# A hand-ordered attention and SwiGLU kernel: its first quarter in another order, its last two project units woven

## The chip, the cores and the metric

One core of one Trainium2 chip. The time is device microseconds of one execution of the program; three executions of the kernel before give the median. TensorE multiplies into PSUM, ScalarE (ACT) and VectorE (DVE) read PSUM and compute element by element, GpSimd (POOL) and SyncE (SP) issue DMAs. In the profile PE is TensorE's matmuls and PEld its weight loads.

## What is computed

Eight batches of attention with eight heads of 576 queries and 64 elements, 16 beacon keys ahead of the 576 causal ones, then a SwiGLU layer on the 4608 tokens of 512 elements:

```python
k_all = np.concatenate([beacon_k, k], axis=2)
v_all = np.concatenate([beacon_v, v], axis=2)
scores = scale * np.matmul(q, k_all.transpose(0, 1, 3, 2))
causal[:, Nb:] = np.triu(np.ones((S, S), dtype=bool), k=1)
scores = np.where(causal, -1000000000.0, scores)
a = np.exp(scores - scores.max(-1, keepdims=True)); a /= a.sum(-1, keepdims=True) + 1e-09
x = np.matmul(a, v_all)            # heads side by side: 4608 x 512
g = x @ w_gate                     # 512 x 1536
out = (g * (1.0 / (1.0 + np.exp(-g))) * (x @ w_val)) @ w_out
```

## The kernel before, in words

Everything is in bf16 with fp32 sums. Matmuls that contract 128 elements are cut into two row halves of 64 partitions, which TensorE takes side by side; `halves` issues them. PSUM is four slots of two banks each. `take` hands the slot that has been free longest to whoever asks next, `give` returns one, so a piece may wait for the piece that had its slot before. Where a bank changes from one row half to the other, `halves` puts a wait for the last matmul of that slot ahead ("one bank, two row halves").

The order of all work is written out by hand, as a string of letters, `plan` (L806). The loop at its end takes a letter after the other and calls `piece`, which issues the next instance of that kind of work; each engine then runs its own instructions in that order. The letters that matter here:

- `l`, a load from the list `order_of_loads`, issued by POOL. The first 24 are free; each later one stands behind a wait for the TensorE work of two pieces before (`passed[-2]`, L739). `K0.4` is batch 0's keys of heads 4 to 7, `K1` all of batch 1's, `Q` the queries, `v1.3` a part of batch 1's values, `g2` and `u2` parts of the gate and value weights (wg, wv), `o0` of w_out, `b1` beacons.
- `f`, `g`: pair_up, a copy of loaded keys and queries into the order that a turn needs, on POOL or on DVE. `T`: a turn, transposes of queries and keys on TensorE. Turns 0 to 4 are of batch 0, 5 to 8 of batch 1, 9 to 12 of batch 2. `K k Q q`: copies of a turn out of PSUM, capitals on DVE, small letters on ACT.
- `S`, `s`: scores of a unit (A to D of a head pair) with, for `s`, the causal mask added on TensorE. `E`: their exponential on ACT, which frees the slot. `D`, `M`: causal masks on DVE or POOL.
- `P`, `p`: product with the values; in batches 0 to 3 with all 128 rows at once. `R`: its normalization on DVE. `X y`: turn and copy of x; `V`: the same by DMA on SP.
- `G`, `H`: the halves of a gate-and-value unit; then tanh on ACT (`a`) and two products on DVE (`1`, `2`). Units 0 to 5 take batch 0's first 240 tokens, 6 to 11 the next 272, later ones 512.
- `F`: a step of the projection with w_out, 24 steps for 256 tokens; `O`, `o`: its copy out of PSUM on DVE or ACT, with the store.
- `h`: a filler. The next scores or product that takes a slot first waits for it, and then issues a pair of matmuls of 128 columns into it for each `h` (`keep_warm`, L176), whose results are overwritten.

The last projection (of the last 256 tokens) is computed in two parts by columns, 0 to 383 and 384 to 511 (`CUT`), each part in slots of its own, one for each bank.

Of the kernel before, what the change touches and what calls it, by code (L numbers as in the profile page):

```python
# [868 lines left out]
```

## Time and profile before

| | us |
|---|---|
| three timed executions | 365.43, 365.43, 364.56 |
| median | 365.43 |
| span of the profiled execution | 362.0 |
| the profiled execution's own time | not listed |
| TensorE busy, matmuls | 352.9 (97%) |
| DVE, ACT, POOL busy | 225.4, 187.6, 124.6 |

The span is the time from the first to the last instruction of one profiled execution. Engines work side by side, so the shares don't add up. Matmuls overlap: a matmul of 512 columns is listed with 0.376 us, and a pair of them starts every 0.216 us, so a busy TensorE is not one at its peak. An idle time in a row stands behind the instruction in brackets, with what ended it.

### The profile page before, as it was taken

What the parts mean: (1) busy time and instruction counts of PE and PEld (TensorE: products, weight loads), DVE (VectorE), ACT (ScalarE), POOL (GpSimd) and SP (SyncE); (2) the same over time, 40 slices, a digit from 0 to 9 for tenths busy, and PEclk for the clock granted to TensorE, in tenths of its full rate; (3) what the DMA queues carried; (4) which work ended last, traced back from release to release, by engine and by line L of the source; (5) the groups of instructions that cost most, each with busy time, mean ns of one, the idle gap of its engine ahead of it and who ended that gap; (6) DMA issues with size and microseconds to landing.
All of it is one profiled execution on the core that took longest, in us unless ns stands there. A gap on an engine that the chain in (4) does not pass through costs nothing.

```text
span 362.0 us, 11888 instructions
## 1 busy us (share of the span) xinstructions
PE 352.9 (97%) x5160; PEld 198.6 (55%) x5160; DVE 225.4 (62%) x439; ACT 187.6 (52%) x284; POOL 124.6 (34%) x188
## 2 busy tenths in 40 slices
PE   7799999999999999999999999999999999999996
PEld 3587565654444566554565566546655554455544
DVE  5577997566766654487528754776467764464342
ACT  4966999723434777544863576447633232221310
POOL 8945499926247545374423013111000000000000
PEclk9999999999999999999999999999999999999999
DMA  8999999999999999999979829502413000110113
GB/s 121 156 197 204 191 191 158 174 175 147 149 147 121 134 136 129 153 174 135 122 132 147 109 37 154 67 6 26 113 62 65 2 2 0 61 60 1 61 60 116
DMA packets 146132, 39.74 MB, mean 110 GB/s; under 512 B 131488, under 2 KB 141728, under 8 KB 146080
## 3 DMA queue, kind: packets, MB, share of 16 engines
q0 software_dynamic: 97424, 19.00, 72.1%
q1 hardware_dynamic: 48368, 19.79, 27.9%
q8 instruction: 40, 0.66, 0.8%
q10 hardware_dynamic: 288, 0.20, 0.2%
q14 instruction: 12, 0.10, 0.1%
...
## 4 chain that ended last, share of the span: by engine, by line
PE 85%; DMA 5%; POOL 5%; DVE 2%; ACT 1%; issue 1%; POOLq 0%
PE gv_ps L168 49%; PE o_ps L168 25%; DMA qk<-in_q_dram 5%; PE s_ps L168 5%; PE pv_ps L168 4%; PE pv_ps L493 2%; POOL qk L209 2%; POOL vb L219 1%; DVE x L522 1%; POOL wg L248 1%; POOL wv L248 1%; DVE p L414 1%; PE t_ps L166 0%; ACT p L405 0%; ACT th L579 0%
## 5 line engine op out<-in xcount | busy, mean ns | idle before, releaser
L168 PE MATMUL gv_ps<-xT,wv 64*128 64x512 bf16 (+2 forms) x912 | 203.2, 365 | 0.0
L168 PE MATMUL gv_ps<-xT,wg 64*128 64x512 bf16 (+2 forms) x912 | 202.8, 365 | 0.1
L579 ACT ACTIVATE th<-gv_ps 128x512 f32<-128x512 f32 (+2 forms) x114 | 65.4, 575 | 116.5 <-PE gv_ps L168 116.1
L405 ACT ACTIVATE p<-s_ps 128x832 bf16<-128x832 f32 (+2 forms) x127 | 104.3, 868 | 32.4 <-PE s_ps L168 28.7
L168 PE MATMUL o_ps<-wo,hT 64*128 64x512 bf16 (+2 forms) x912 | 116.5, 365 | 0.2
L584 DVE SCALAR_TENSOR_TENSOR u<-th,gv_ps 128x512 f32<-128x512 f32 (+2 forms) x114 | 74.7, 656 | 65.9 <-ACT th L579 65.1
L168 PEld LDWEIGHTS <-wg 64*128 64x128 bf16 x912 | 82.5, 94 | 45.9 <-PE gv_ps L168 2.4
L168 PEld LDWEIGHTS <-wv 64*128 64x128 bf16 x912 | 81.8, 94 | 40.1 <-issue 0.7
L591 DVE SCALAR_TENSOR_TENSOR hT<-gv_ps,u 128x512 bf16<-128x512 f32 (+2 forms) x114 | 74.7, 661 | 3.0
L168 PEld LDWEIGHTS <-hT 64*128 64x128 bf16 x912 | 42.3, 94 | 34.1 <-PE o_ps L168 1.2
L219 POOL DMA_DIRECT2D vb<-in_v_dram x40 | 33.9, 853 | 64.1 <-PE s_ps L168 25.7
L168 PE MATMUL s_ps<-qT,kT 64*128 64x336 bf16 (+3 forms) x512 | 43.0, 250 | 1.9 <-ACT kT L256 1.0
L168 PEld LDWEIGHTS <-kT 64*128 64x128 bf16 x512 | 23.8, 94 | 22.9 <-ACT kT L256 1.8
L219 POOL DMA_DIRECT2D qk<-in_q_dram x25 | 21.2, 851 | 25.7 <-PE gv_ps L168 7.1
L414 DVE TENSOR_TENSOR p<-p,upper 128x256 bf16<-128x256 bf16 (+2 forms) x84 | 24.0, 317 | 9.8 <-ACT p L405 8.1
L522 DVE TENSOR_TENSOR x<-pv_ps,rec 128x640 bf16<-128x640 f32 (+1 forms) x32 | 25.3, 791 | 1.2
L521 DVE RECIPROCAL rec<-pv_ps 128x10 f32<-128x10 f32 (+1 forms) x32 | 6.8, 213 | 28.1 <-PE pv_ps L168 22.7
L258 DVE COPY o_sb<-o_ps 128x512 f32<-128x512 f32 (+2 forms) x20 | 12.7, 654 | 17.0 <-PE o_ps L168 13.9
L219 POOL DMA_DIRECT2D qk<-in_k_dram x25 | 21.3, 856 | 5.4 <-PE gv_ps L168 4.3
L418 POOL TENSOR_SCALAR_AFFINE_SELECT p<-p 128x256 bf16<-128x256 bf16 (+2 forms) x46 | 17.4, 399 | 14.0 <-ACT p L405 13.8
L168 PEld LDWEIGHTS <-p 64*128 64x128 bf16 x960 | 18.8, 94 | 4.5 <-PE pv_ps L168 0.2
L168 PE MATMUL pv_ps<-vb,p 64*128 64x65 bf16 x960 | 19.9, 189 | 0.0
...
## 6 DMA issues: line engine op xcount, KB each, us to landing
...
```

What stands on the lines that cost most here:

```text
L168: ins = nc.tensor.matmul(o, lhsT=l, rhs=r, start=start, stop=stop)
L209: return nc.gpsimd.dma_start(qk[b % 2][base : base + HALF, RUN * h0 : RUN * h1] .rearrange("p (h e) -> p h e", e=RUN)[:, :, D * i0 : D * i ...
L219: return nc.gpsimd.dma_start(dst[p0 : p0 + n, c, :, 0:D], src[b, :, r : r + n, :].rearrange("h j d -> j h d"))
L248: nc.gpsimd.dma_start(t[:, :, cols], src[:, cols].rearrange("(kk p) f -> p kk f", p=P))
L258: eng.tensor_copy(o, i)
L405: nc.scalar.activation(p_of(b, m, u == "A")[:, :, c0 : c0 + w], ps[:, :, 0:w], ACT.Exp, scale=0.125)
L414: nc.vector.tensor_tensor(out=ap, in0=ap, in1=upper[:, None, d : d + w].to_broadcast([P, 2, w]), op=ALU.mult)
L418: nc.gpsimd.affine_select(out=ap, in_=ap, compare_op=ALU.is_ge, fill=0.0, base=d, pattern=[[0, 2], [1, w]], channel_multiplier=-1,)
L522: nc.vector.tensor_tensor(out=xs[b][:, c0:NKT, P * m : P * m + P].rearrange("p c (h d) -> p h c d", d=D), in0=o[:, :, :, 0:D], in1=rec[:, ...
L579: nc.scalar.activation(th[:, 0:w], gvs[n][:, 0, 0:w], ACT.Tanh, scale=0.5)
L584: nc.vector.scalar_tensor_tensor(out=u[:, 0:w], in0=ths[n][:, 0:w], scalar=1.0, in1=gvs[n][:, 0, 0:w], op0=ALU.add, op1=ALU.mult)
L591: nc.vector.scalar_tensor_tensor(out=hTs[j][:, f, c0:c1], in0=gvs.pop(n)[:, 1, 0 : c1 - c0], scalar=0.5, in1=ths.pop(n)[:, 0 : c1 - c0], o ...
```

## The change

The fixed number of free loads goes; a new letter `L` is a free load, `l` always a paced one. The list of loads is reordered up to about its fiftieth entry. The plan is another one up to gate-and-value unit 23 (0-based), with the same pieces but 38 fillers in place of 10, and with some copies, masks and pair_ups on another engine (`A` and `Y` are beacon and x copies on DVE). After that the letters are the same up to the copies behind the last two project units, numbers 16 and 17, each of 24 steps. These two are woven: first half of 16, first half of 17's part 0, second half of 16, first half of 17's part 1, second half of part 0, second half of part 1. Part 0 now has 320 columns, and the two parts of 17 share a slot, one in each bank; for unit 17 the wait of `halves` looks at the bank alone and not at the slot.

```diff
@@ -50,7 +50,6 @@
 W_PARTS = [(0, 1), (1, 3), (3, 6), (6, 9), (9, 12)]
 
 
-FREE_LOADS = 24
 
 NHT = 2
 NPT = 3
@@ -151,16 +150,17 @@
     newest = [None]
     passed = []
 
-    def halves(key, bank, row, o, l, r, start, stop, turn=False):
+    def halves(key, bank, row, o, l, r, start, stop, turn=False, alone=False):
 
         at = (held[key], bank)
         was = writers.get(at)
         if was is not None and was[0] != row:
-            last = max((w for (i, _), w in writers.items() if i == at[0]), key=lambda w: w[2])
+            near = [w for w in writers if (w == at if alone else w[0] == at[0])]
+            last = max((writers[w] for w in near), key=lambda w: w[2])
             if was[3]:
                 after(nc.tensor.nop(), last[1], "one bank, two row halves")
             for other, w in writers.items():
-                if other[0] == at[0]:
+                if other in near:
                     writers[other] = (w[0], w[1], w[2], False)
         if turn:
             ins = nc.tensor.transpose(o, l, r)
@@ -595,33 +595,39 @@
         give(("g", n))
 
     projected = {}
-    CUT = 384
+    CUT = 320
+    LAST = NCH * 2 - 1
+    PARTS = (slice(0, CUT), slice(CUT, DM))
+
+    steps = [(pr, 0, f) for pr in range(LAST - 1) for f in range(2 * NF)]
+    for pr, part, half in (
+        (LAST - 1, 0, 0), (LAST, 0, 0), (LAST - 1, 0, 1), (LAST, 1, 0), (LAST, 0, 1), (LAST, 1, 1)
+    ):
+        each = 2 if pr == LAST else 1
+        steps += [(pr, part, f) for f in range(NF * half, NF * half + NF, each)]
 
     def project(n):
-        pr, s = divmod(n, 2 * NF)
+        pr, part, s = steps[n]
         j, i = divmod(2 * pr, TOK // P)
-        last = pr == NCH * 2 - 1
-        parts = [(0, slice(0, DM), s)]
-        if last:
-
-            parts = [(0, slice(0, CUT), 2 * s), (0, slice(0, CUT), 2 * s + 1)] if s < NF else [
-                (1, slice(CUT, DM), 2 * (s - NF)), (1, slice(CUT, DM), 2 * (s - NF) + 1)]
-        for part, cols, st in parts:
-            if st == 0:
+        last = pr == LAST
+        cols = PARTS[part] if last else slice(0, DM)
+        for st in range(s, s + 1 + last):
+            if st == 0 and part == 0:
                 for bank in range(2):
-                    key = ("f", pr, part, bank * last)
+                    key = ("f", pr, bank * last)
                     if key not in held:
                         ps = take(key, [P, 2, DM], FP32, "o_ps")
-                    projected[pr, part, bank] = key, ps
+                    projected[pr, bank] = key, ps
             second, f = divmod(st, NF)
             for row in (1, 0) if second else (0, 1):
                 bank = row ^ second
-                key, ps = projected[pr, part, bank]
+                key, ps = projected[pr, bank]
                 k64 = slice(HALF * row, HALF * row + HALF)
+                at = part if last else bank
                 halves(
-                    key, bank, row, ps[:, bank, cols],
+                    key, at, row, ps[:, at, cols],
                     hTs[j][k64, f, P * (i + bank) : P * (i + bank) + P], wo[k64, f, cols],
-                    st == 0, st == 2 * NF - 1,
+                    st == 0, st == 2 * NF - 1, alone=last,
                 )
 
     stored = {}
@@ -629,17 +635,17 @@
     def evacuate(n, eng):
 
         pr, bank = divmod(n, 2)
-        part, cols = 0, slice(0, DM)
-        if pr >= NCH * 2 - 1:
-            part, cols = pr - (NCH * 2 - 1), (slice(0, CUT), slice(CUT, DM))[pr - (NCH * 2 - 1)]
-            pr = NCH * 2 - 1
+        part, cols, at = 0, slice(0, DM), bank
+        if pr >= LAST:
+            part = at = pr - LAST
+            pr, cols = LAST, PARTS[part]
         r = 2 * P * pr + P * bank
         if part == 0:
             stored[pr, bank] = o_pool.tile([P, DM], FP32, name="o_sb")
         o_sb = stored[pr, bank]
-        key, ps = projected[pr, part, bank]
-        copy(eng, o_sb[:, cols], ps[:, bank, cols])
-        if bank == 1 or key[-1] != projected[pr, part, 1][0][-1]:
+        key, ps = projected[pr, bank]
+        copy(eng, o_sb[:, cols], ps[:, at, cols])
+        if part if pr == LAST else bank:
             give(key)
         (nc.sync if part == 0 or bank == 0 else nc.scalar).dma_start(out[r : r + P, cols], o_sb[:, cols])
 
@@ -718,24 +724,23 @@
         named[f"K0.{h}"] = lambda h=h: runs(0, k, h, h + 4, FRONT, ROWS)
         named[f"Q0.{h}"] = lambda h=h: runs(0, q, h, h + 4, FRONT, ROWS)
     order_of_loads = """
...
     """
     loads = [named[name] for name in order_of_loads.split()]
     assert sorted(order_of_loads.split()) == sorted(named)
     turns = [load for b in range(NPE, B) for load in dma_transposes(b)]
 
     def piece(kind):
-        as_kind = {"s": "S", "M": "D", "k": "K", "q": "Q", "Y": "y", "o": "O", "i": "I", "A": "e", "f": "g"}.get(kind, kind)
+        as_kind = {"s": "S", "M": "D", "k": "K", "q": "Q", "Y": "y", "o": "O", "i": "I", "A": "e", "f": "g", "L": "l"}.get(kind, kind)
         n = done.get(as_kind, 0)
         done[as_kind] = n + 1
-        if kind == "l":
-            if n >= FREE_LOADS:
-
+        if kind in "lL":
+            if kind == "l":
                 after(nc.gpsimd.nop(), passed[-2], "paced load")
             loads[n]()
         elif kind == "b":
@@ -804,25 +809,25 @@
     skipped = [0]
 
     plan = """
-    0lhbTqllhhWKeBhTQslTlEKlsqlkElhhSlTQsKElKEslssUQEshsEhDElshEEEllhlTQZkNZsNSPpJEEIlsJPllERIpSXlDR
...
-    FFFOFFFFOFFFOFFFFOFFFFFFFFOo
+    bLWLB0TQLTkAhhsETqKsqKhhSEThhhsLEELQKkLhsEhsQELhhhsTLQsLELKLELhhsEhhhZhhsUDhZNLhshhhSELsLNJIEhhS
...
+    FFFF1FFFFF2oFFFFFFFFFFFFOFFFFFFFOFoFFFFFFFFFFFOoFFFFFFOo
     """
```

At the start, DVE's first work behind the memsets (before, then after; `first` is the first loaded keys and queries, `beacons` the beacon keys, `t_ps` a turn's result):

```order
L258 CAST qk_101<-first 128x256 [waits DMAHW1_49,DMAHW0_49]
L270 CAST beacons_98<-first_beacons 16x512 [waits DMAHW2_49,DVE_49]
L258 COPY kT_107<-t_ps 128x256 [waits Activation_49]
L258 COPY qT_105<-t_ps 128x256 [waits PE_49]
L258 COPY kT_107<-t_ps 128x256
L258 COPY qT_105<-t_ps 128x320 [waits PE_49]
```

```order
L270 CAST beacons_98<-first_beacons 16x512 [waits DMAHW2_49,DVE_49]
L258 CAST qk_101<-first 128x256 [waits DMAHW1_49,DMAHW0_49]
L258 COPY qT_105<-t_ps 128x256 [waits PE_49]
L258 COPY kT_107<-t_ps 128x4x16
L258 COPY kT_107<-t_ps 128x256 [waits PE_49,Activation_49]
L258 COPY kT_107<-t_ps 128x2x256 [waits Activation_49]
```

The cast of the beacons now stands ahead of the cast of `first`, and the copy of the turned beacons is DVE's.

POOL's queue around the first pair_up of batch 1 (`side<-qk`; `wg`, `wv` weights, `vb` values, `qk` keys and queries, `p` the mask's operand), before and after:

```order
L248 DMA wv<-in_moe_w_val_dram 128x4x384 [waits DMASW7_49]
L248 DMA wg<-in_moe_w_gate_dram 128x4x384 [waits DMASW0_49]
L248 DMA wg<-in_moe_w_gate_dram 128x4x384 [waits DMASW1_49]
L248 DMA wv<-in_moe_w_val_dram 128x4x384 [waits DMASW2_49]
L258 COPY side<-qk_102 128x1152 [waits DMASW5_49,DMASW4_49]
L209 DMA qk_101<-in_q_dram 64x8x576 [waits DVE_49,DMASW3_49,PE_49,Activation_49]
L219 DMA vb_104<-in_v_dram 80x8x64 [waits PE_49]
```

```order
L418 AFFINE_SELECT p_109<-p_109 128x2x128 [waits Activation_49]
L248 DMA wg<-in_moe_w_gate_dram 128x4x384 [waits DMASW7_49]
L248 DMA wv<-in_moe_w_val_dram 128x4x384 [waits DMASW0_49]
L248 DMA wv<-in_moe_w_val_dram 128x4x384 [waits DMASW1_49]
L219 DMA vb_104<-in_v_dram 112x8x64 [waits PE_49,DMASW2_49]
L258 COPY side<-qk_102 128x1152 [waits DMASW5_49,DMASW4_49]
L219 DMA vb_104<-in_v_dram 128x8x64 [waits PE_49,DMASW3_49]
L248 DMA wg<-in_moe_w_gate_dram 128x4x384
L219 DMA vb_104<-in_beacon_v_dram 16x8x64 [waits PE_49]
L258 COPY side<-qk_102 128x1152
L209 DMA qk_101<-in_q_dram 64x8x576 [waits DMASW6_49,DVE_49]
L209 DMA qk_101<-in_k_dram 64x8x576 [waits PE_49,DMASW7_49]
```

A mask now stands ahead of three weight loads, one weight load behind the first pair_up, and two pair_ups ahead of the loads of batch 2.

TensorE in the last unit, where the second half of its last part begins, before and after (`o_ps` a slot, `hT` the activated tokens):

```order
L168 LDWEIGHTS hT
L168 MATMUL o_ps<-wo,hT 128x128
L168 LDWEIGHTS hT [waits PE_49]
L168 MATMUL o_ps<-wo,hT 128x128
L168 LDWEIGHTS hT [waits PE_49]
L168 MATMUL o_ps<-wo,hT 128x128
```

```order
L168 LDWEIGHTS hT
L168 MATMUL o_ps<-wo,hT 128x320
L168 LDWEIGHTS hT [waits PE_49]
L168 MATMUL o_ps<-wo,hT 128x192 [waits DVE_49]
L168 LDWEIGHTS hT [waits PE_49]
L168 MATMUL o_ps<-wo,hT 128x192 [waits Activation_49]
L168 LDWEIGHTS hT
```

Before, the weight loads wait for TensorE's own matmuls just ahead; now the matmuls wait for DVE and ACT as well.

## Rows read from the trace of the kernel before

**Rows 1.** Busy time of engines by stretch; columns are in its first line

```profile
core 0: us, PE busy (x) PEld busy (x) DVE busy (x) ACT busy (x) POOL busy (x), PEclk, DMA share, GB/s
5.00:20.00 15.00, 11.79 (x361) 8.92 (x359) 7.96 (x22) 12.17 (x18) 14.85 (x23) 1.00 1.57 156
20.00:32.50 12.50, 12.32 (x236) 10.16 (x232) 9.51 (x27) 7.37 (x17) 3.25 (x5) 1.00 1.27 204
32.50:49.50 17.00, 16.77 (x285) 9.96 (x286) 15.39 (x30) 15.61 (x26) 11.03 (x15) 1.00 1.69 189
...
82.00:350.00 268.00, 267.95 (x3602) 143.08 (x3598) 163.69 (x294) 128.37 (x190) 66.06 (x100) 1.00 0.84 90
```

**Rows 2.** Chain of waits, 15 to 60 us: start us, us, what

```profile
17.83 13.37 DMA qk<-in_q_dram
...
31.35 1.15 POOL side L258
...
33.68 0.76 ACT kT L256 x2
```

**Rows 3.** The last wv load of units 3 to 5: its issue and landing

```profile
L248 POOL DMA_DIRECT2D wv<-in_moe_w_val_dram x1: 770/770/770, 16.4 to 16.4; - x1
...
DMA to landing us min/median/max: 9.0/9.0/9.0
```

**Rows 4.** TensorE in order of time: unit 3's start, and turn 5

```profile
25.62 0.26 PE L168 MATMUL gv_ps<-xT,wg 64*128 64x240 bf16 x1
...
32.55 0.44 PE L166 MATMUL t_ps<-ident,side 64*128 64x64 bf16 x18 [0.22 <-POOL side L258]
```

**Rows 5.** Chain of waits over the whole span, one long piece

```profile
79.46 13.92 PE gv_ps L168 x128
```

**Rows 6.** DVE and TensorE in order of time, first 7 us

```profile
4.44 0.52 DVE L258 CAST qk<-first 128x256 bf16<-128x256 f32 x1 [0.35 <-DMA first<-in_k_dram]
5.06 0.64 DVE L270 CAST beacons<-first_beacons 16x512 bf16<-16x512 f32 x1
...
5.42 0.32 PE L166 MATMUL t_ps<-ident,qk 64*64 64x64 bf16 x16
```

**Rows 7.** The first beacons: issue, and time to landing

```profile
L653 SPq DMA_DIRECT2D first_beacons<-in_beacon_k_dram x1: 830/830/830, 1.6 to 1.6; - x1
...
DMA to landing us min/median/max: 3.4/3.4/3.4
```

**Rows 8.** ACT in order of time, exponentials of batch 0

```profile
11.54 4.80 ACT L405 ACTIVATE p<-s_ps 128x832 bf16<-128x832 f32 x6
...
23.20 0.89 ACT L405 ACTIVATE p<-s_ps 128x832 bf16<-128x832 f32 x1
```

**Rows 9.** TensorE in order of time, first value products of batch 1

```profile
49.65 1.35 PE L493 MATMUL pv_ps<-vb,p 128*128 128x65 bf16 x39
51.22 0.36 PE L493 MATMUL pv_ps<-vb,p 128*128 128x65 bf16 x6 [0.22 <-POOL p L418]
51.51 0.33 PE L168 MATMUL s_ps<-qT,kT 64*128 64x240 bf16 x4
51.77 0.62 PE L493 MATMUL pv_ps<-vb,p 128*128 128x65 bf16 x15
```

**Rows 10.** Chain of waits, 345 us to the end

```profile
350.01 4.76 PE o_ps L168 x48
...
354.79 2.87 PE o_ps L168 x48
...
357.67 0.89 PE o_ps L168 x24
```

**Rows 11.** TensorE groups by shape: the last projection's first part

```profile
L168 PE MATMUL o_ps<-wo,hT 64*128 64x384 bf16 x48 | 4.3, 323 | 0.1
```

**Rows 12.** DVE in order of time, last copies

```profile
356.94 1.02 DVE L258 COPY o_sb<-o_ps 128x384 f32<-128x384 f32 x2 [2.84 <-PE o_ps L168]
358.55 0.29 DVE L258 COPY o_sb<-o_ps 128x128 f32<-128x128 f32 x1 [0.58 <-PE o_ps L168]
```

More of the change, by code (lines that the diff above doesn't have):

```diff
@@ L720 @@
     order_of_loads = """
-    K0.0 Q0.0 v0.2 Q0.4 K0.4 v0.1 v0.0 v0.3 v0.4 v0.5 g1 u0 g0 u1 g2 u2 K1 Q1 b1 u3 g3 g4 u4 Q2 v1.5 K2 v1.3 v1.2
-    v1.0 v1.1 v1.4 b2 o0 o1 v2.2 k3.0 v2.1 q3.2 v2.5 k3.5 v2.4 v2.3 v2.0 q3.4 q3.0 q4.2 k4.0 v3.3 k3.1 q4.0 k3.4
-    k3.2 q3.1 v3.0 k4.2 q3.3 k4.3 v3.5 q4.4 k3.3 v3.4 v3.2 k4.5 k4.1 q4.3 q4.1 v4.1 v4.5 v4.3 v4.0 k4.4 v3.1 v4.2
-    q6.1 k5.0 q5.1 q5.4 k5.3 k5.5 k6.0 k5.2 k5.1 q5.0 k6.2 q5.3 v4.4 k6.1 q6.0 q6.2 k6.5 q5.2 v5.2 k5.4 k7.0 k7.2
-    v5.5 q7.1 k6.3 k7.1 v5.1 q7.2 k7.4 q7.3 q6.3 v5.4 k6.4 q6.4 k7.5 v5.0 k7.3 v5.3 q7.4 q7.0 v6.0 v6.1 v6.2 v6.4
-    v6.3 v6.5 v7.4 v7.5 v7.2 v7.1 v7.3 v7.0
+    Q0.0 K0.0 Q0.4 K0.4 v0.1 v0.2 v0.0 u1 v0.5 v0.3 v0.4 u0 g0 g1 u2 g2 Q1 K1 b1 g3 u3 u4 v1.1 v1.2 g4 v1.0 Q2
+    K2 v1.3 b2 v1.4 v1.5 o0 o1 v2.5 v2.1 q3.3 v2.0 v2.3 v2.4 v2.2 k3.0 k3.1 k3.2 q3.0 q3.1 q4.2 v3.3 k4.0 v3.0
+    k4.3 k4.2 k3.5 q4.4 q4.0 k3.4 v3.5 q3.4 q3.2 k3.3 v3.4 v3.2 k4.5 k4.1 q4.3 q4.1 v4.1 v4.5 v4.3 v4.0 k4.4
+    v3.1 v4.2 q6.1 k5.0 q5.1 q5.4 k5.3 k5.5 k6.0 k5.2 k5.1 q5.0 k6.2 q5.3 v4.4 k6.1 q6.0 q6.2 k6.5 q5.2 v5.2
+    k5.4 k7.0 k7.2 v5.5 q7.1 k6.3 k7.1 v5.1 q7.2 k7.4 q7.3 q6.3 v5.4 k6.4 q6.4 k7.5 v5.0 k7.3 v5.3 q7.4 q7.0
+    v6.0 v6.1 v6.2 v6.4 v6.3 v6.5 v7.4 v7.5 v7.2 v7.1 v7.3 v7.0
     """
@@ L812 @@
-    ll2ltGHal1G2lGHHa1aatlt21tGH1H2lattF2aGFH112FF2FFGSaEFlHt1GFFaHa2Gltl1t2GtlH12latH12Fa12FFGGtDHS
-    ltlaE1FHFFaG2lSFHtl12allF12GFElMFllFHaSG1FEFHaGFFolMHl2l1G2aSOF1H2FaE1FtFG2sHFEaFslF1FDFlSE2FDFE
-    DFSESlPpFFFRlDFFFlStFESSDFFEFFsEDFOPEpMPEOpSFFlFRMStRFEFEFSsFEMEFFDFFPplFSFFFFFlFRDSSEFEtFtSFDFF
-    FFFEEFlVFFsoOElFFSFtFFDFtSMPEDEtSFElpSDRFFMFFtlMPtESSFEEpRFttFFGFDDSEGHFGa12HHlla1aG21FHl2aGlFHl
-    1a2GSHD1ool2aDtPlEGM1ltp2HRlla1GtlSlGH2alEGHG1l2FaM1HHF2a1GFa2HS1FF2FSFFaEFSFEF12lFSPEFpDMFEFSlS
@@ L822 @@
-    Ha1a12HG2Ga1H122HGa1Ga2G1HHH2aa1a21G21GH2aG12HaHGFFFF1a2FFGF1H2aHaGF1H2FaF1GF2F1GHHFFFaa2FF12G1G
-    HaFFFFH12F2FFFFFFaG1FHFFoFaFoFF212GGFHaFF1FHFF2FFaFGFFFFOHoG12GHHFaa12GFaFFF1FFF21FHF2GGFFaHFaFF
-    1FFF12FHa2FG1GFHF2HFaF1FoaFFoFFFFFG2FF1FFHFaF1FGFF2HGFFFaFF12FH2FFaFFFFF1FFFFF2oFFFFFFFFFFFFOFFF
-    FFFOFFFFOFFFOFFFFOFFFFFFFFOo
+    bLWLB0TQLTkAhhsETqKsqKhhSEThhhsLEELQKkLhsEhsQELhhhsTLQsLELKLELhhsEhhhZhhsUDhZNLhshhhSELsLNJIEhhS
+    EEJPpDIhPpEhhSRLRhhSDhhPLEEGpLDHLGMaR1X2hPLLHLYlpGXRyHXYGGHaf1aa2X1HlL2Gy1l2GHHa1G2GfLaH1a212GaH
@@ new lines @@
+    a1HGa212TqKHlla12GSEHhhSa1Gfl2sElT12lHEKalSGQSHE1lTgMMEaq212GMhhSHkSlGMEsaEHD12ESETQfaGKSfHSEM12
+    DlaGsEEH1aTql2MMk12SlPplEsPsRDEpSERPpFfSEFSFFFESlREDEFlPTkpSFlqFDDDFFFFlTRESSVFFFFFQEKFSSDEMDlFF
+    FFFEFSOlFFFFFEEgSFElMFMDFOTttFFQFMFSStFFFlkEMEFFPpPDplPRRpFFFFFRlFFSlEoOsMGlGlESHGESalD12EDHallH
+    aP1Gtpl2RHGllla1l2G1HHGVa21lll2ltGHal1G2lGHHa1aatlt21tGH1H2lattF2aGFH112FF2FFGSaEFlHt1GFFaHa2Glt
+    l1t2GtlH12latH12Fa12FFGGtDHSltlaE1FHFFaG2lSFHtl12allF12GFElMFllFHaSG1FEFHaGFFolMHl2l1G2aSOF1H2Fa
@@ new lines @@
+    E1FtFG2sHFEaFslF1FDFlSE2FDFEDFSESlPpFFFRlDFFFlStFESSDFFEFFsEDFOPEpMPEOpSFFlFRMStRFEFEFSsFEMEFFDF
+    FPplFSFFFFFlFRDSSEFEtFtSFDFFFFFEEFlVFFsoOElFFSFtFFDFtSMPEDEtSFElpSDRFFMFFtlMPtESSFEEpRFttFFGFDDS
+    EGHFGa12HHlla1aG21FHl2aGlFHl1a2GSHD1ool2aDtPlEGM1ltp2HRlla1GtlSlGH2alEGHG1l2FaM1HHF2a1GFa2HS1FF2
+    FSFFaEFSFEF12lFSPEFpDMFEFSlSRFFlEFFtSFttEFFDFSFVFFESEtFFFMsMDEFFFDFEsOFSFFolPttDEFDFSpFFEMFsESFR
+    FFFEFFtFPMEGGOtHoSEtaplHRPtla11Gpt2HD2tGMRaGSt1HH2tGEa1al2G1HSa2GEH1a2GttHGa12SHH1a2MEG1GaM2DSHH
@@ new lines @@
+    ES12FaEFFFFF1FDla2FFPSF1FE2FpRFFSFFSEFSFESFFFFVEFSFFFFDDFEFFEFFDSoFPFFMlFpFEStlFERFFFFFSSDoEPMFF
+    EFFFDDOMGpoRSElPHGa1S2pHEaR1G2sHlGGEDaHaD12GG1Ha2H12aG1Ha2HaGG12S1EHlHGa2a1D2MSH1FEl2GSMFa1H2EMP
+    aFDF1FSF2EDFFFpSFEFFsRFFFSFFFSEFPEEFFSFpERFFSFFFMDVFMSFFDEEPFFDSoFFFFpFFFFEFDOFSPRFDFSpEGFFFEGRG
+    DDFHaO1oHH2aa12P1GpRHGGH2VaGHa1a12HG2Ga1H122HGa1Ga2G1HHH2aa1a21G21GH2aG12HaHGFFFF1a2FFGF1H2aHaGF
+    1H2FaF1GF2F1GHHFFFaa2FF12G1GHaFFFFH12F2FFFFFFaG1FHFFoFaFoFF212GGFHaFF1FHFF2FFaFGFFFFOHoG12GHHFaa
@@ L826 @@
+    12GFaFFF1FFF21FHF2GGFFaHFaFF1FFF12FHa2FG1GFHF2HFaF1FoaFFoFFFFFG2FF1FFHFaF1FGFF2HGFFFaFF12FH2FFaF
+    FFFF1FFFFF2oFFFFFFFFFFFFOFFFFFFFOFoFFFFFFFFFFFOoFFFFFFOo
     """
```

9 lines of the change are left out of this document (removed).

## The prediction

> **What bounds the kernel now.** I read the page first: a span of 362.0 us, most of it TensorE's. The timed executions have a median of 365.43 us, so about 3.4 us lie around the span; the profiled execution's own time is not listed, and I add every change of the span to the median. What a measurement of this kernel can tell from no change is taken as 0.3%, 1.1 us.
>
> Then the table by stretches [rows 1]. From 82 us to 350 us TensorE is busy for 267.95 of 268.00 us. The lists that the change orders anew end at gate-and-value unit 23, which TensorE starts at about 82 us, and what follows is the same list until the last 48 project steps. So the middle is a fixed length: the end moves one for one with the time at which TensorE arrives at unit 23, plus what the tail does. In the first three stretches TensorE is not the only limit. From 5 to 20 us it is busy for 11.79 of 15 us, and POOL, which issues the loads, for 14.85. The granted clock is 1.00 in every one of them, so there is no slow clock to win back.
>
> Then the chain of waits [rows 2]. It runs for 13.37 us through one load (batch 1's queries, issued at 17.83), then through POOL's pair_up of that load (1.15 us), and only then through TensorE's turn 5 at 32.55. The same is true at an earlier point: the last wv load that units 3 to 5 need is issued at 16.41 and lands 9.0 us later, at 25.4 [rows 3], and unit 3 starts at 25.62 [rows 4]. So up to turn 5 the loads set the pace; TensorE is merely on time for them.
>
> **Price list.** 128 matmuls of 512 columns take 13.92 us, so a pair (two row halves at once) costs 0.217 us [rows 5]; I scale with the columns: 0.163 us at 384, 0.136 at 320, 0.083 at 192, 0.056 at 128, 0.116 at 272. A filler pair is two matmuls of 128 columns: 0.056 us.
>
> **Part 1, up to turn 5.** The number of filler letters grows from 10 to 38; 24 of the 28 new pairs stand before turn 5 (1.34 us) and 4 behind (0.22 us). On DVE the cast of the beacons now stands ahead of the cast that the first turn needs. Before, the first began at 4.44 and the second at 5.06 [rows 6]; now the beacons' DMA is waited for first (issued at 1.6, landed 3.4 later, at 5.0 [rows 7]), then 0.64 and 0.52 us of casts follow, so the first turn starts near 6.3 instead of 5.42, some 0.85 us later. Against that, POOL selects "below" before the v load that preceded it, and ACT loses two of the copies between its exponentials. ACT has 16 exponentials here, at 0.80 us each (six in 4.80), the last ending at 24.1 before [rows 8]. Walking the new order by hand from a first one at 7.8 us (16 at 0.80 to 0.82, three copies of some 0.5, one gap of about 1 us for want of a PSUM slot) the last ends near 23. That gives back the late start, and the fillers of this stretch stand in waits of TensorE.
>
> The first 16 free loads are the same set in another order, and so are the first 18. They moved at 156 GB/s from 5 to 20 us and at 204 from 20 to 32.5 [rows 1]. A queue that is never empty lands a set at the same time in any order, so I keep 25.4 us for the last weights of units 3 to 5 and 31.2 us for the batch-1 pair. If loading weights earlier fills holes in the first stretch it could be up to 0.5 us earlier; if POOL, whose mask now stands ahead of three loads, were late, up to 0.5 us later.
>
> From unit 3 to turn 5 the new list has one gate half more (unit 10's, 4 pairs of 272 columns: 0.46 us). Before, TensorE was through with that stretch at about 32.2 (idle 0.22 us before turn 5 by the row [rows 4], and some 0.15 us more, since the row counts the last matmuls' whole length); now it arrives at 32.2 + 0.46 = 32.65. Turn 5 is 0.1 us later, with 0.46 us of work done ahead and 0.22 us of fillers still to come: 0.10 - 0.46 + 0.22 = **-0.14 us**. Ends: -0.7 (loads 0.5 earlier) and +1.3 (the 24 fillers all on the path).
>
> **Part 2, turn 5 to the first value product of batch 1.** Before, ACT copied both halves of turn 5 one after the other, with kT ending at 34.44 [rows 2]; now DVE copies kT beside ACT's qT, which frees the first scores by 0.3 us. But more slots now come free late: gate unit 12 takes the slot that the exponential of A0 leaves, about 0.8 us behind its scores, and unit 16 that of D1. By the price list the old order has 16.1 us of matmuls between 32.55 and 49.65 [rows 9], so 1.0 us of waits and changes; the new one has 16.0 us, and my walk finds six waits of 0.1 to 0.25 us and the same changes, 1.5 us together. Two fewer pair_ups on DVE, busy 15.39 of 17 us here [rows 1], speak for less. Between 0.5 more and somewhat less I take **+0.2 us**, with ends -0.8 (all of the old waits go) and +0.9.
>
> **Part 3, to unit 23.** Each change between 128-row value products and 64-row work costs TensorE about 0.1 us: the scores at 51.51 need 0.16 us for two pairs and the product follows at 51.77 [rows 9], and the way back costs the same. The old list has 6 groups of value products in batches 1 and 2, the new one 9: 3 x 0.2 = +0.6 us. Gone are the wait for POOL's mask at 51.22 (0.22 us in the row) and, as an estimate, 0.3 us of smaller ones; new is one behind the copies of turn 9, which ACT does one after the other ahead of B3's scores. I take **+0.1 us**, ends -0.8 and +1.0.
>
> **Part 4, the tail.** Each of the last two units changes row halves in one bank, and the new half waits for the old one to drain. The chain shows the three places [rows 10]: from 350.01, 12 pairs of 512 and 12 of 384 columns are 4.55 us, yet the next piece starts at 354.79, 0.23 us late; from there 12 x 0.163 + 12 x 0.056 = 2.63 us, and the next starts at 357.67, 0.25 us late; the first, at 350.01, cost 0.24. The weave puts other work between the halves, so 0.72 us goes. What is late next is in the order rows: the last six steps write the second bank of tiles whose first bank is being copied out, and their first matmul waits for DVE, the other bank's for ACT. The copy cannot start before the last 320-column matmul has ended (0.30 us, where 384 columns take 0.32 [rows 11]); DVE takes 0.49 us for 320 columns (0.29 for 128, 0.51 from one to the next at 384 [rows 12]); the wake-up is 0.05, as from POOL's end at 32.50 [rows 2] to the turn at 32.55 [rows 4]. Without the wait the next pair would have started 0.14 us after the last: 0.30 + 0.49 + 0.05 - 0.14 = 0.70 us of new wait. The final copy has 192 columns instead of 128: +0.07. Sum: 0.70 - 0.72 + 0.07 = **+0.05 us**, ends -0.6 (the wait costs nothing) and +0.3.
>
> The Trainium skill, "PSUM — Partial Sum Buffer", section Terms, has engines collide only in the same bank; by that the chip would not need this wait, and the tail would be 0.70 us shorter. No row here shows a copy and a matmul in two banks of one tile; the wait stands in the program whether the chip needs it or not.
>
> Sum: -0.14 + 0.2 + 0.1 + 0.05 = +0.2 us. **Forecast 365.65 us, no change that can be measured.**
>
> **Rivals.** *Faster.* The loads land 0.5 us earlier, and the new order has neither the old waits of parts 2 and 3 (1.0 and 0.5 us) nor the price of its three extra groups: -0.7 - 0.6 - 0.5 = -1.8, 363.6 us. For it: POOL is saturated to 20 us and DVE nearly so from 32 to 49 us, and the change relieves DVE. Against it: the loads' total is unchanged, and between 20 and 82 us TensorE is already near full. Chance 0.27.
>
> *Slower.* Before turn 5 TensorE, no longer the loads, is last: the fillers stand behind the wait for a slot and ahead of the scores, so each adds 0.056 us to the chain slot, scores, exponential, slot. It decides from the point where ACT's last exponential of batch 0 ends later than about 22.3 us, for then unit 3 comes after 25.5. My walk has 23.0, a breach of 0.7 us that I take to be the error of the walk; if all 24 count and the late start with them, turn 5 is at 33.9: +1.3, 366.8 us or somewhat above. Chance 0.25.
>
> *The tail does what its shape says*, with no wait left: 365.65 - 0.70 = 364.95. That is inside no change, and the waits in the order rows speak against it; it has 0.05 of the 0.48 of the middle case.
>
> The Trainium skill, "TensorE: Matmul & The Clock Gate", section Why this matters for your kernels, warns that idle gaps of TensorE in mid-kernel halve its clock; by that more fillers could keep runs from a slow stretch, and the faster rival would gain. Here the granted clock is 1.00 in all early stretches with the ten fillers of before, and three timed runs lie within 0.87 us, so I give it nothing.
>
> **How the numbers follow.** No change (364.3 to 366.5) 0.48, faster 0.27, slower 0.25. The forecast's own range, from its ends in part, is 364.5 to 366.6. The range for 8 in 10 reaches to the centres of the rivals and a little beyond: 363.7 to 367.2.
>
> **What will show it.** Turn 5's first matmul between 32.4 and 32.9 (the load pair still the releaser of POOL's pair_up at about 31.3): part 1 right; after 33.5 with no load as releaser: the slower rival; before 32.2: the faster one. The first value product of batch 1 near 50.2. Unit 23 near 82.2. In the tail, one idle time of TensorE of about 0.7 us ahead of the first 192-column matmul, with DVE's copy as releaser, and none at the three old places. I am wrong if unit 23 starts more than 1 us from 82, if the clock falls below 1.00 before 350 us, or if the tail's new wait is under 0.4 us.

## The result, and the profile after

| | before | changed |
|---|---|---|
| median, us (11 runs each) | 365.41 | 367.55 |
| lowest to highest | 364.18 to 367.05 | 366.29 to 369.24 |
| ratio, 95% interval | | 1.0067 (1.0052 to 1.0083) |
| profiled execution, span | 362.0 | 367.5 (its time 369.24) |

The change makes the kernel 0.67% slower, 2.1 us by the medians. The forecast was 365.65, and the range ended at 367.2.

Five executions further down, one of them of before, took 396 to 939 us; the ratios are without these.

The spans differ by 5.5 us, far more than the times. The profiled execution of the changed kernel lasted 369.24 us with a span of 367.5, so 1.74 us lie around a span, not the 3.4 that the prediction took. By that the profiled execution of before lasted about 363.7 us (an estimate), 1.7 under its median, and that of the changed kernel 1.7 above its own. Differences of these two profiles are therefore read beside other executions, below.

First the table by stretches of the changed kernel, columns as in [rows 1]:

```profile
5.00:20.00 15.00, 12.08 (x343) 9.23 (x342) 7.72 (x20) 10.27 (x16) 14.21 (x21) 1.00 1.59 157
20.00:32.50 12.50, 11.55 (x228) 8.69 (x226) 7.63 (x22) 5.93 (x11) 3.48 (x5) 1.00 1.32 199
32.50:49.50 17.00, 16.27 (x284) 11.19 (x280) 13.97 (x30) 12.24 (x23) 14.19 (x21) 1.00 1.58 183
87.21:350.00 262.79, 262.79 (x3556) 142.61 (x3554) 160.71 (x289) 126.69 (x187) 68.47 (x103) 1.00 0.90 91
```

From unit 23, now at 87.21 us, TensorE is busy without a break, as before. Ahead of it the table alone doesn't tell what is late: ACT and DVE are busy for less of these stretches than before, partly because the work comes later.

The chain of waits, 20 to 40 us, which before ran through a load and POOL's pair_up [rows 2] (start us, us, what):

```profile
20.31 0.31 issue
...
25.14 0.93 PE gv_ps L168 x16
26.07 0.26 PE xt_ps L536 x3
26.32 0.16 PE pv_ps L182
26.48 0.63 issue
27.12 0.21 PE pv_ps L182
27.33 0.47 PE pv_ps L493 x12
27.80 0.52 PE gv_ps L168 x8
28.32 0.47 PE pv_ps L493 x12
28.78 0.52 PE gv_ps L168 x8
29.30 0.26 PE xt_ps L536 x3
...
32.00 5.51 PE gv_ps L168 x96
37.51 0.29 PE t_ps L166 x19
...
37.92 0.66 ACT qT L256
...
38.61 0.87 DVE kT L258 x2
...
39.52 0.33 PE s_ps L168 x4
```

No load stands in it, only TensorE behind itself, until the copies of turn 5 (and two stalls, 0.31 and 0.63 us, called "issue", for which the profile shows no reason). POOL's pair_up for that turn, in order of time:

```profile
33.03 1.14 POOL L258 COPY side<-qk 128x1152 bf16<-128x1152 bf16 x1 [3.81 <-DMA qk<-in_k_dram]
```

It ends at 34.17, 3.2 us before turn 5 starts at 37.35. Before, it ended at 32.50 and the turn followed at 32.55 [rows 2, 4]. So the bound of this stage has gone from the loads to TensorE.

ACT's last exponentials of batch 0, in order of time, in the changed kernel and then in a run whose letters are the same up to turn 5 (k5_on_act, below):

```profile
23.39 1.70 ACT L405 ACTIVATE p<-s_ps 128x928 bf16<-128x928 f32 x2 [0.55 <-PE s_ps L168]
```

```profile
21.32 1.70 ACT L405 ACTIVATE p<-s_ps 128x928 bf16<-128x928 f32 x2 [0.55 <-PE s_ps L168]
```

They end at 25.1 and at 23.0; the walk in the prediction had 23. Half of the difference comes from the start, half from TensorE's lower clock up to about 14 us (below). In the chain of waits from 0 us of the changed kernel the first turn hangs on the beacons' load, issued at 1.61:

```profile
1.61 3.77 DMA first_beacons<-in_beacon_k_dram
```

It took 3.0 to 3.9 us in the profiles of this study, 3.4 in [rows 7] and 3.1 in k5_on_act, whose first turn began 1.0 us sooner.

The tail, in order of time:

```profile
362.06 0.49 DVE L258 COPY o_sb<-o_ps 128x320 f32<-128x320 f32 x1 [1.92 <-PE o_ps L168]
362.09 0.44 ACT L256 ACTIVATE o_sb<-o_ps 128x320 f32<-128x320 f32 x1 [1.32 <-PE o_ps L168]
...
362.60 1.17 PE L168 MATMUL o_ps<-wo,hT 64*128 64x192 bf16 x24 [0.58 <-DVE o_sb L258]
...
363.79 0.36 DVE L258 COPY o_sb<-o_ps 128x192 f32<-128x192 f32 x1 [1.24 <-PE o_ps L168]
```

The last 24 matmuls wait for DVE's copy. From start to start, less the price of the columns, the wait is 0.76 us; the three late starts of [rows 10] are gone.

### The profile page after: what moved, and what is told of

Read it like the earlier page. It is cut to its first block, busy times and chain, and to the rows that moved or that the text cites. A ratio compares the mean times of both kernels' runs of the same rounds, so it can differ in the third digit from the quotient of the medians.

```text
span 367.5 us, 12001 instructions
## 1 busy us (share of the span) xinstructions
PE 356.5 (97%) x5216; PEld 204.6 (56%) x5216; DVE 223.4 (61%) x435; ACT 186.6 (51%) x281; POOL 128.5 (35%) x195
## 4 chain that ended last, share of the span: by engine, by line
PE 93%; DVE 2%; ACT 2%; DMA 1%; issue 1%; SPq 0%; DVEq 0%; ACTq 0%
PE gv_ps L168 51%; PE o_ps L168 26%; PE s_ps L168 7%; PE pv_ps L493 4%; PE pv_ps L168 4%; PE t_ps L166 1%; DMA first_beacons<-in_beacon_k_dram 1%; ACT p L405 0%; DVE kT L258 0%; PE s_ps L182 0%; DVE x L453 0%; ACT qT L256 0%; DVE qT L258 0%; DVE o_sb L258 0%; PE xt_ps L536 0%
## 5 line engine op out<-in xcount | busy, mean ns | idle before, releaser
L168 PEld LDWEIGHTS <-hT 64*128 64x128 bf16 x912 | 43.6, 94 | 33.6 <-PE o_ps L168 0.8
L414 DVE TENSOR_TENSOR p<-p,upper 128x256 bf16<-128x256 bf16 (+2 forms) x78 | 20.3, 289 | 10.9 <-ACT p L405 10.4
L418 POOL TENSOR_SCALAR_AFFINE_SELECT p<-p 128x256 bf16<-128x256 bf16 (+2 forms) x52 | 19.8, 404 | 18.6 <-ACT p L405 18.3
L258 DVE COPY o_sb<-o_ps 128x512 f32<-128x512 f32 (+2 forms) x17 | 11.1, 657 | 21.3 <-PE o_ps L168 16.4
```

The lines of the kernel that those rows point to most:

```text
L168: ins = nc.tensor.matmul(o, lhsT=l, rhs=r, start=start, stop=stop)
L258: eng.tensor_copy(o, i)
L414: nc.vector.tensor_tensor(out=ap, in0=ap, in1=upper[:, None, d : d + w].to_broadcast([P, 2, w]), op=ALU.mult)
L418: nc.gpsimd.affine_select(out=ap, in_=ap, compare_op=ALU.is_ge, fill=0.0, base=d, pattern=[[0, 2], [1, w]], channel_multiplier=-1,)
```

## The experiments

Theory F: the added filler pairs lie on TensorE's path, and each costs its 0.056 us. Theory O: they stand in waits, and the new order costs (its start, its copies, its row changes). Theory C: TensorE's clock is lower at the start. The times below are medians; the ratio is to before, run beside it, and its 95% interval stands in brackets. The next table holds places read from the traces, where the matmuls of a piece begin (us; the last column is a length):

| | turn 0 | unit 3 | turn 5 | unit 23 | turn 5 to 23 |
|---|---|---|---|---|---|
| before | 5.42 | 25.62 | 32.55 | 81.99 | 49.44 |
| tail_only (same letters so far) | 5.49 | 25.67 | 32.54 | 83.38 | 50.84 |
| tail_cover (same letters so far) | 5.48 | 25.74 | 33.06 | 83.91 | 50.85 |
| fill_only | 5.48 | 27.19 | 33.73 | 83.42 | 49.69 |
| changed | 6.53 | 30.26 | 37.35 | 87.21 | 49.86 |
| head_only (same letters so far) | 5.98 | 28.82 | 35.90 | 85.76 | 49.86 |
| k5_on_act (same to turn 5) | 5.50 | 27.63 | 34.71 | 84.33 | 49.62 |
| few_fillers | 6.43 | 27.70 | 34.78 | 84.64 | 49.86 |
| late_out | 5.97 | 27.57 | 34.66 | 84.52 | 49.86 |
| early_out | 5.67 | 28.13 | 35.21 | 85.08 | 49.87 |
| chain_few | 6.45 | 26.98 | 34.07 | 83.93 | 49.86 |
| head_mended | 5.02 | 25.93 | 33.02 | 83.34 | 50.32 |
| pool_only | 5.02 | 26.72 | 33.26 | 82.36 | 49.10 |

The letters of before come to turn 5 between 32.54 and 33.78 us in six profiles (pool_relief and pool_weave are the two not in the table). In five of the six a load paces them, for the turn follows POOL's pair_up by 0.05 to 0.06 us; in pool_only TensorE came last. Those of the changed head come between 34.71 and 37.35 in three, where TensorE carries a late start on.

**Head or tail.** tail_only: the letters and loads of before, the weave of the change. head_only: the reverse.

> The head of before (its letters, its loads) with the woven tail of after. If the tail is neutral, as its two halves in the trace of after say (0.72 us of three row changes gone, one wait of 0.76 us for DVE's copy come), the time is 365.4 us within 0.4, and the 2.1 us are all in the head. If the tail costs what the chance allowed, up to +0.3, it is 365.7. If the weave costs more than the wait shows, about 366.5 or above.

> The head of after (letters up to the last two project units, loads) with the tail of before. If the loss is all in the head: 367.5 us, with turn 5 several us later than 32.55 and the three row changes of 0.24, 0.23 and 0.25 us back at the end. If the tail carries half of it: 366.5.

tail_only 365.52 us, 1.0007 (0.9992 to 1.0022); head_only 368.25, 1.0076 (1.0051 to 1.0102). The loss is in the head, and none that can be told from nothing is in the tail. The profiles say a little more of the tail. From unit 23 to TensorE's end it takes 276.55 us in before and in tail_only alike, but the span goes on for 3.45 us behind that in before and for 3.72 in tail_only.

**Fillers.**

```diff
 fill_only: before, fillers ahead of the scores and products up to turn 5
-  A0 4, A2 2, C1 1, pv_front 0 2, D1 1
+  A0 2, A2 2, A3 3, B0 1, C0 1, D0 3, C1 2, pv_front 0 3, D1 2, pv_front 1 1, B2 1, C2 3, B3 2,
+  P m1 1, C3 2, D3 2, P m2 2, P m3 1
 few_fillers: after, with the first line; no_fillers: before, with none
```

> Before with the filler pairs of after ahead of the same scores and value products up to turn 5: 34 pairs in place of 10, nothing else moved. Theory F, the fillers are on the path of TensorE: 24 x 0.056 = 1.3 us, turn 5 near 33.9 and the time 366.7. Theory O, the fillers stand in waits that are there anyway and the new order costs: turn 5 at 32.5 to 32.8 as before, the time 365.4 to 365.7.

> After with the filler counts of before up to turn 5, 10 pairs in place of 34, nothing else moved. Theory F: 367.55 - 1.3 = 366.2 us. Theory O: 367.2 to 367.6, with turn 5 still near 37 us. If both count, between.

> Before without its ten filler pairs up to turn 5, nothing else changed. Theory F, a pair costs TensorE what it takes: 10 x 0.056 = 0.56 us less, but turn 5 can't come earlier than the load and its pair_up let it (32.1 to 32.5), so 364.5 to 365.0 us. If the fillers hold the granted clock up in the waits of the start: a clock under 1.00 before 20 us, and a time above 365.5.

A row change is a change of TensorE between 128-row and 64-row work, which part 3 of the prediction prices at 0.1 us.

fill_only 366.30, 1.0031 (1.0016 to 1.0046): 24 pairs alone cost 1.2 us, and turn 5 comes 1.2 us later. few_fillers 365.92, 1.0024 (1.0004 to 1.0044): without them the change loses 0.24% in place of 0.67; the difference is 1.6 us. Theory F holds on both sides: the pairs lie on TensorE's path, at about their price of 1.34. Part of what they cost is row changes, for some stand ahead of value products: up to turn 5 before has 15 of them, few_fillers 23, the changed kernel 27. By the prices 24 pairs and four changes are 1.74 us, an estimate, against the 1.6 measured.

no_fillers 365.47, 1.0010 (0.9990 to 1.0030): no gain, though ten pairs have a price of 0.56 us. Its table by stretches (columns as in [rows 1]) holds a possible reason:

```profile
14.00:17.80 3.80, 2.53 (x84) 1.98 (x80) 2.38 (x8) 3.70 (x5) 3.52 (x5) 1.00 1.58 156
17.80:21.20 3.40, 3.40 (x51) 2.63 (x52) 1.06 (x4) 2.00 (x3) 3.40 (x6) 0.50 1.27 156
21.20:24.00 2.80, 2.80 (x70) 2.27 (x68) 2.13 (x7) 1.90 (x4) 1.09 (x3) 1.00 1.25 184
```

Behind a stretch with TensorE busy 2.53 of 3.80 us, the granted clock is 0.50 (1.2 GHz) through the next one, and turn 5 comes at 34.13, though there are ten pairs less. Before has 1.00 there. One profile doesn't show that the ten fillers would have prevented it: three kernels with these fillers fall to 0.50 as well, between 10 and 15 us (below).

**Which fillers.** late_out: after without the 16 added pairs behind the first front product; early_out: without the 8 ahead of it.

> After with the filler counts of before behind the first front product, that is without 16 of the 24 added pairs, all issued between 16 and 28 us. If TensorE is itself the bound from about 16 us on, each costs its 0.056 us: -0.9, 366.6 us. If the late ones stand in waits: 367.4 or more, and it is the early ones that cost.

> After with the filler counts of before up to the first front product, without 8 of the 24 added pairs, all issued before 16 us. If every pair costs its length: -0.45, 367.1 us. If the early ones stand in waits for copies and exponentials: 367.4 to 367.6, or above, if the lower clock then lasts longer.

late_out 366.43, 1.0034 (1.0020 to 1.0048): 1.2 us back. The 16 pairs have a price of 0.9, and the four row changes that go with them one of 0.4. early_out 367.82, 1.0067 (1.0041 to 1.0094): nothing back that can be told, but its profile has the lower clock from 8.8 to 12.2 us, so it doesn't settle what the first eight pairs cost. fill_only and tail_only, both at the higher clock from 7.3 us on, tell more: the first value product of batch 0 starts at 15.31 and 15.08, so eight pairs cost 0.23 us up to there, half their price; at unit 3 fill_only is 1.52 us late. So the waits of the first 16 us hold about half of their fillers, and the pairs issued from there on are what costs most. From 16 us to turn 5 TensorE has few waits left beside its row changes (in head_only's profile one of 0.13 us and one stall of 0.33); the pairs lengthen its own work.

**The start and TensorE's clock.**

```diff
 start_as_before, plan
-bLWLB0TQLTkAhhsE
+0LbTQLBWLTkAhhsE
 k5_on_act, turn 5
-TqKH
+TqkH
 chain_short, turn 1's query copy on DVE
-LTkAhhsETqKsqK
+LTQkAhhsETKsqK
 waits_filled
-LTkAhhsETqKsqK
+LTkAhhhhhhhhsETqKhhhhhhhhhhhhsqK
 warm_long
-    warm(8, TOK)
+    warm(10, TOK)
```

> After with the start of before: the cast of the loaded keys and queries ahead of the cast of the beacons, turn 0 ahead of the beacons' turn, below selected where before had it among the loads. If the late start is carried through to the end: the first exponential ends near 8.4 us in place of 9.4, turn 5 comes 0.8 to 1.1 us earlier, and the time is 366.5 to 366.8. If the stage is bound by ACT and the slots whatever the start, or by the beacons' own landing: 367.2 to 367.6.

> After with the key copy of turn 5 on ACT, behind its query copy, as before; one letter. Theory S, two engines that copy one slot go one after the other by the program's waits (in the trace of after DVE's copy begins when ACT's ends, and the first scores of batch 1 wait 0.87 us): the wait shrinks to under 0.2 us and the time falls by 0.7 to 0.9 to about 366.7 us. Rival, what is late is TensorE's own work or the copy's length: the wait stays above 0.5 us or comes back at the next scores, and the time stays at 367.5.

> After with one copy moved: turn 1's query copy on DVE, right behind turn 0's, in place of ACT behind the first exponential. In the traces of after's head the second scores wait 1.26 to 1.41 us for that copy, in those of before's head they don't wait. Theory C, what the new start costs is the wait, and through it TensorE's clock: in four of five profiles of that head the matmuls up to about 14 to 16 us start at the spacing of the lower clock, in those of before's head only up to 7.5. Then the wait falls under 0.4 us, the higher clock comes or stays more often, and the time is 366.2 to 366.8. Theory F, only the fillers count: 367.4 to 367.7, the wait moves to the next scores.

> After with 18 filler pairs more, 6 ahead of the first scores and 12 ahead of the second, where TensorE waits 0.66 and 1.26 us. Theory C: they stand in waits and cost nothing there, the clock is up by 8 us and stays, and the time falls to 366.3 to 366.8. Theory F, each pair costs what it takes: 367.55 + 1.0 = 368.5. If both are wrong, 367.5.

> After with 10 in place of 8 long warm-up matmuls, so that TensorE has no pause before the beacons' turn; they end about 0.85 us later, near 6.4, some 0.2 us behind the landing of most runs. If that pause is what keeps the clock down: the higher clock by 8 us in the profile and 366.4 to 367.0. If it is the waits behind (0.66 and 1.26 us): still the lower clock up to 14 us, and 367.6 to 368.

start_as_before 367.54, 1.0066 (1.0043 to 1.0090): no gain; in its profile the beacons landed 3.8 us after their issue, and the second scores still began at 9.42, behind ACT's query copy. k5_on_act 367.74, 1.0070 (1.0042 to 1.0098): the first scores of batch 1 wait 0.63 in place of 0.87 us, now for ACT. My theory S falls: what they wait for is the length of the two copies, 0.66 and 0.87 us in the chain above, with one gate half (0.46 us) less work between turn 5 and the scores than before. chain_short 367.05, 1.0060 (1.0040 to 1.0080): the second scores start at 7.84 in place of 8.8 to 10.2, but the third then wait 1.1 us; the time is not clear of the change's. warm_long 367.76, 1.0065 (1.0045 to 1.0086): nothing.

waits_filled 368.42, 1.0097 (1.0075 to 1.0119). Its median is 0.9 us above the change's, about the 1.0 that the pairs cost in all, though the two intervals overlap. That goes against theory C, the more so as its profile has the higher clock from 7 us on. Its profile doesn't show such a price where the pairs stand: from turn 0 to turn 5 it takes 29.47 us, chain_short 29.23 and k5_on_act 29.21. It loses 0.85 us between gate units 40 and 50, where nothing was changed. What its median shows stays open.

The clock at the start is told by the matmuls. Matmuls of 240 columns from 9 to 12 us in before, in the changed kernel and in head_only (busy us, mean ns of one; idle before):

```profile
L168 PE MATMUL s_ps<-qT,kT 64*128 64x240 bf16 x4 | 0.6, 273 | 0.7 <-ACT kT L256 0.7
```

```profile
L168 PE MATMUL s_ps<-qT,kT 64*128 64x240 bf16 x4 | 0.8, 378 | 1.0 <-ACT qT L256 1.0
```

```profile
L168 PE MATMUL s_ps<-qT,kT 64*128 64x240 bf16 x6 | 1.2, 386 | 1.2 <-ACT qT L256 1.2
```

And the row of that stretch in head_only, then in the changed kernel:

```profile
9.00:12.00 3.00, 2.69 (x80) 2.13 (x82) 1.66 (x4) 1.74 (x3) 3.00 (x5) 0.50 1.71 166
```

```profile
9.00:12.00 3.00, 1.96 (x75) 1.37 (x64) 1.12 (x2) 2.19 (x5) 3.00 (x5) 1.00 1.56 151
```

The changed kernel's column says 1.00, but its matmuls take what they take in head_only at 0.50: it runs at 1.2 GHz there. By the same measure it does so up to about 14 us, head_only from 8.4 to 15, start_as_before up to 14, k5_on_act and chain_short not at all behind 5.5. Before and the kernels with its head and ten fillers are at the higher level by 7.5 us, and three of them, pool_relief, pool_only and pool_weave, fall once more, somewhere between 10 and 15 us, though their letters up to there are before's. The Trainium skill, "TensorE: Matmul & The Clock Gate", section Part 1: The HAM clock gate, says that the same kernel can warm up at another point in each run; the executions here agree. What the lower level costs can be read where the letters are the same. The first turn, and the fillers ahead of the first value product, in k5_on_act, then in the changed kernel:

```profile
5.50 0.46 PE L166 MATMUL t_ps<-ident,qk 64*64 64x64 bf16 x32
14.46 0.34 PE L182 MATMUL pvf_ps<-ident 64*128 64x128 bf16 x6 [0.21 <-ACT p L405]
```

```profile
6.53 0.65 PE L166 MATMUL t_ps<-ident,qk 64*64 64x64 bf16 x32
16.64 0.34 PE L182 MATMUL pvf_ps<-ident 64*128 64x128 bf16 x6 [0.21 <-ACT p L405]
```

From one to the other it takes 8.96 us at the higher level and 10.11 at the lower. So in this one pair of profiles, of the 2.64 us between them at turn 5, 1.03 are the start, 1.15 come with the clock, and the rest is about the stalls called "issue". The medians don't settle how often that happens: chain_short, with the higher clock in its profile, is 0.5 us under the change, inside the intervals.

**What is left without the fillers.** chain_few is chain_short with ten fillers; head_mended has besides the old start and two products not cut by gates:

```diff
-PLEEGpLDHLGMaR1X2PLLHLYlpGXRyHXY
+PpLEEGHLDGLMaR1X2PpLLHLYlRGXyHXY
```

> chain_short with the filler counts of before up to turn 5. Theory F alone: as with the fillers taken out before, 365.9 to 366.1. Theory C and F together: 365.0 to 365.4, as before, if the clock is kept; if ten fillers don't keep it with this order, 365.9 or more with the lower clock between 6 and 16 us.

> After with the ten fillers of before, the start of before (cast of the loaded keys first, turn 0 ahead of the beacons' turn), turn 1's query copy on DVE, and the value products of two pairs not cut by gates, so with four row changes less. If start and row changes are the remaining 0.8 us: 365.0 us within 0.3. If the remainder lies behind turn 5: 365.7 or more.

chain_few 365.79, 1.0020 (1.0003 to 1.0036); head_mended 365.51, 1.0021 (1.0005 to 1.0036). In its profile head_mended is at unit 23 at 83.34, level with tail_only, and yet its time stays 0.2% above before. Start and the copy's engine are not what is left. Row changes may be a part: chain_few still has 23 up to turn 5 and head_mended 19, where before has 15. The tail's end may be another. But the interval of head_mended overlaps that of tail_only; what these 0.5 to 0.8 us are, no run here shows.

**Waits that only the old list has.** The tail in another order, and two masks of batch 1 on DVE:

```diff
 tail_cover, order of the last pieces (unit, part, half)
-16.0.0, 17.0.0, 16.0.1, 17.1.0, 17.0.1, 17.1.1
+16.0.0, 17.0.0, 17.1.0, 17.0.1, 16.0.1, 17.1.1
 pool_only, before's plan
-ElSEMDlTGMSQaKEHSMM12
+ElSEDDlTGDSQaKEHSMM12
 pool_relief = both; pool_weave = pool_only, tail 16.0.0, 17.0.0, 16.0.1, 17.0.1, 17.1.0, 17.1.1 in separate slots
```

> The head of before, and the woven tail in another order: unit 16 first half, unit 17 part 0 first half, part 1 first half, part 0 second half, then unit 16's second half, then part 1's second half; the copies of part 0 come ahead of those of unit 16. The 2.6 us of unit 16's second half stand between the copies of part 0 and the matmuls that waited for them. Expected: no wait of 0.76 us and none at the row changes, TensorE's end 0.7 us earlier; the time 364.6 to 364.8 if the last store is what ends the run, but 365.1 or more if the two big stores of unit 16, now issued at the end, delay the last small ones.

> The head of before with two masks of batch 1 on DVE in place of POOL, and the tail in which unit 16's second half covers the copies. In two of three profiles of that head the products of batch 1 wait 1.1 us for POOL's masks near 51 us, behind loads. If these waits are on the path: they go, and the time is 363.9 to 364.3. If POOL's other work (turn 9's pair_up) takes their place: 364.8 to 365.0.

> Before with two masks of batch 1 on DVE in place of POOL, nothing else. If the 1.1 us of waits for POOL's masks near 51 us are on the path and the tail in the other order was worth nothing: 364.4 to 364.7 us. If the tail brought pool_relief's 0.4 us: 365.0.

> pool_only with the last two units woven so that each part keeps slots of its own: unit 16 first half, unit 17 part 0 first half, 16 second half, 17 part 0 second half, then part 1, first and second half, 384 and 128 columns as before. Two of the three waits at row changes (0.24 and 0.23 us) have other work between them, the third (0.25 us) stays, no copy stands between matmuls, and unit 16's stores come early. Expected: 0.47 us below pool_only, about 364.1; if the slots for part 1 come late, as much as pool_only.

tail_cover 364.95, 1.0002 (0.9985 to 1.0018). The wait of 0.76 us is gone, but the chain of waits ends with the copies of unit 16, which now come last:

```profile
358.75 0.70 DVE o_sb L258
...
359.48 0.31 ACT o_sb L256
...
359.97 0.32 ACT o_sb L256
```

TensorE ends at 359.69, the span at 364.1, 4.4 us later; in before it is 3.45. What TensorE saves, the last stores take.

What TensorE waits for from 45 to 60 us in tail_cover (head of before; us in total, times, longest), and then in pool_only:

```profile
PE pv_ps L493 <- POOL p L418: 0.8, 2, 0.5
PE t_ps L166 <- DMA beacons<-in_beacon_k_dram: 0.4, 1, 0.4
PE s_ps L168 <- DVE x L522: 0.2, 1, 0.2
```

```profile
PE pv_ps L493 <- issue: 0.3, 1, 0.3
```

The waits go. From turn 5 to unit 23 pool_only takes 49.10 us against 50.85, but pool_weave, with the same masks on DVE, took 50.12, and before itself 49.44, so these profiles don't show what the masks are worth. The times: pool_only 364.80, 0.9993 (0.9978 to 1.0009); pool_relief 364.58, 0.9992 (0.9975 to 1.0010); pool_weave 364.91, 0.9988 (0.9969 to 1.0006). All three medians lie below before, none clear of it. No version here is shown to beat before.

## Why the prediction was wrong

**Around the span.** It took 3.4 us between span and median; 1.7 to 2.1 is what nearly all executions on record show, and the rest is that the profiled execution of before was a short one: its span of 362.0 us is near the lower end of the spans of before, 361.9 to 366.3. Its stretch from turn 5 to unit 23 took 49.44 us; two other executions of the same letters took 50.84 and 50.85, with waits for POOL's masks (0.8 us from 45 to 60 us in each) that the page read for the prediction hardly shows (0.22 us in [rows 9]).

**Part 1 is the step that failed**: turn 5 at 32.65, "the fillers of this stretch stand in waits of TensorE". Turn 5 came at 34.7 to 37.35. What held it up was TensorE's own work, not a load: POOL's pair_up began at 33.03 in the changed kernel, 1.7 us later than assumed, and at 30.86 in head_only, and either way it ended before TensorE was free. The chain before did show a load at its end [rows 2], with TensorE through with its own work at 32.2, 0.35 us before the turn: a stage that near to two bounds has no room for 1.8 us more work. The prediction even had the sign: ACT's last exponential at 23.0 where 22.3 was the point from which TensorE is last, "a breach of 0.7 us that I take to be the error of the walk". It was no error: k5_on_act shows 23.0, and that with a start at 5.50 where the walk assumed 6.3. The start itself differed between executions: turn 0 came at 6.53 in the changed kernel, at 5.98 in head_only, at 5.50 in k5_on_act, 0.1 to 1.1 us later than before's 5.42, and the prediction's 0.85 lies between. And up to turn 5 the list has 27 row changes where before had 15, with gaps of 0.09 to 0.11 us in both traces. Four of them come with the added fillers. The other eight make 0.8 us, an estimate, near the 0.24% (0.9 us) that few_fillers still loses; no run takes them out alone, so that part of the loss is argued, not shown. Such changes were priced in part 3 but left out of part 1. The Trainium skill, "TensorEngine Tiling (Array Packing)", section Key Properties, says that a change of tiling mode drains TensorE; the gaps of 0.09 to 0.11 us agree.

**The slower rival** (0.25, 366.8 us) has the mechanism that the runs show: turn 5 behind TensorE with no load as releaser, and 1.3 us for the 24 pairs against 1.2 measured alone and 1.6 inside the change. Its time is 0.75 us short of 367.55. Its sentence names the late start too, but its sum leaves it out; with 0.85 for that it would have been 367.6, which would have been luck, since the start moved by 1 us between executions and the row changes were not counted. And it counted all 24 pairs at full price; it is mostly the late 16 that show.

**Part 2**: from turn 5 to the first product 17.55 us were predicted, 17.45 measured. The size was right as far as one profile tells (the old letters took 17.1 to 17.9), the reason half wrong: DVE's key copy did not free the first scores by 0.3 us, they waited 0.87 for it. **Part 3**: from there to unit 23 32.41 us against 32.34 before, +0.07 where +0.1 was taken; against two other executions of the old letters (33.0 each) it is a gain of 0.6, so the size is not told more closely than that. The new list takes 49.6 to 49.9 us from turn 5 to unit 23 in all profiles but one, the old one 49.4 to 50.9. The 4.8 us between the profiles of before and of the change at turn 5 are 5.2 at unit 23 and 5.5 at the end; 3.4 of these are the lengths of the two executions, 1.7 under and 1.7 above their medians, which leaves 2.1.

**Part 4** was right on TensorE: a wait of 0.76 us (0.70 predicted) for the three of 0.72 together, and 1.0007 in tail_only. It left out the time from TensorE's end to the span's, 0.3 us longer with the weave in the profiles and inside the interval of tail_only. That TensorE needs no such wait, as the rival on the tail had it, was not tried: the wait stands in the program.

**The faster rival** had nothing: up to turn 5 TensorE was last in the changed kernel, so neither earlier loads nor less work on POOL and DVE could have been worth anything there.
